# Pairing the 64-row low-weight passes of two column groups on the two row halves of TensorE

## The chip, the cores and the metric

The kernel runs on one core of a Trainium2 chip. The metric is the device time in microseconds of one execution. Engines: PE (TensorE, matmul), PEld (its weight loads, which overlap PE), DVE (VectorE), ACT (ScalarE), POOL (GpSimd) and SP (the queue that issues most transfers).

## The reference

An adaptive layer norm block over 2048 tokens of 576 channels: a long convolution (S4D), then a feed-forward network with a hidden width of 4608. Cut to what matters:

```python
def _B_ref(x, w1, w2):
    h = jnp.einsum("bsd,df->bsf", x, w1)
    zero = jnp.zeros_like(h)
    h = jnp.maximum(h, zero)
    return jnp.einsum("bsf,fd->bsd", h, w2)

x = A_u
mod = (_silu(c) @ w_mod).reshape(c.shape[0], 6, 1, -1)
sa, ca, ga, sb, cb, gb = (mod[:, 0], mod[:, 1], mod[:, 2], mod[:, 3], mod[:, 4], mod[:, 5])
h = _layernorm(x, axis=-1) * (1 + ca) + sa
x = x + ga * _A_ref(h, A_log_A_real, A_A_imag, A_C_real, A_C_imag, A_log_dt, A_D_skip)
h = _layernorm(x, axis=-1) * (1 + cb) + sb
x = x + gb * _B_ref(h, B_w1, B_w2)
return x
```

`_A_ref` is the convolution with a kernel of 2048 taps for each channel, done with FFTs. Everything is float32.

## The kernel before

**Stages.** The kernel first makes the convolution's taps and the first block's convolution (`conv0`). From about 209 us on it works on four blocks of 512 tokens: the feed-forward network of block b runs on PE, and between its passes stand, in portions, the convolution and norm of block b+1 (generators that `step`, L1405, advances four times per column group: once inside `first`, once after it, once inside `second`, once at the end of the iteration). A portion holds up to some 2.7 us of DVE work by the kernel's own figures. DVE, ACT and PE each run their instructions in the order in which they were issued; a scheduler orders them by program order and by when they become ready in its own model.

**Feed-forward.** The hidden width is cut into 36 column groups of 128, so there are 4 × 36 = 144 groups g. For each, `first(g)` (L1362) makes the 128 × 512 sum `hps` (hidden columns × tokens) and `second(g)` (L1379), two iterations later, multiplies it by w2 into five accumulators. To keep float32 accuracy, both operands are split into a high and a low part in fp32r, and three products are made: high × high, high weight × low activation, low weight × high activation.

**The tail of 64 channels.** 576 is 4 × 128 + 64. For the four full chunks `first` runs three passes each. The host stores the last 64 rows of w1 twice, in partitions 0 to 63 and 64 to 127 of the fifth chunk; `norm2` (L1074) makes the activations of those channels in both halves too. The tile `xs` holds the high part in partitions 0 to 63 and the low part in 64 to 127 (L1128 to L1132). So one pass with the high weights, over all 128 rows, makes high × high and high × low at once. The second pass, with the low weights, is over 128 rows as well. That is 14 passes per group: 2 with `xs`, 12 with `xh` and `xl`.

**After the sum.** ACT makes `hh = relu(hps)` (L1375), DVE makes `hl = max(hps, 0) − hh` (L1376). `hps` has two buffers, so `first(g + 2)` can't start before `hl(g)` has read its own. `hh` and `hl` have three buffers each.

**Weights.** `load_r1` and `load_r2` (L1319 and on) bring the raw weights; ACT makes the high parts (`split1`, L1337; `split2`, L1350), DVE the low parts in block 0, which are saved to DRAM; later blocks load them back (`low1`, L1327, for w1; in `split2` for w2). The buffers of `w1` are three; that of group g was free after `first(g)`, and `low1(g + 3)` was issued there. The transfers go through SP's queue in program order.

Of the kernel before, what the change touches and what calls it, by code (L numbers as in the profile page):

```python
# [10 lines left out]
F32 = mybir.dt.float32  # L11
F32R = mybir.dt.float32r
I32 = mybir.dt.int32
AF = mybir.ActivationFunctionType
ALU = mybir.AluOpType
# [3 lines left out]
P = 128  # L19
# [5 lines left out]
NF = F // P  # L25
# [503 lines left out]
class Body:  # L529
# [20 lines left out]
    def v(self, *args, **kw):  # L550
        return self.kept(self.nc.vector.tensor_tensor(*args, **kw))  # L551
# [522 lines left out]
    def norm2(self, s, x2, xp, st=None):  # L1074

        nc, v = self.nc, self.nc.vector.tensor_tensor
        xh = xp.tile([P, 4, 512], F32R, tag="xh", bufs=1, name=f"xh_{s}")
        xl = xp.tile([P, 4, 512], F32R, tag="xl", bufs=1, name=f"xl_{s}")
        xs = xp.tile([P, 512], F32R, tag="xs", bufs=1, name=f"xs_{s}")
        self.xT[s] = (xh, xl, xs)  # L1080
        if st is None:
            st = self.sums("st2")
            for p in range(2):
                yield from self.stats(
                    lambda i: x2[:, i, p * PC : (p + 1) * PC], [t[:, p] for t in st]
                )
        rs = self.norms(st, False)
        yield 2.0
        if s == 0:
            h2 = [self.cv.tile([P, D + 64], F32, tag="h2", bufs=4, name="h2") for _ in range(4)]  # L1090
        else:
            h2 = [
                t[:, i * (D + 64) : (i + 1) * (D + 64)]
                for t in (self.spec(f"h2_{i}").rearrange("p a b c -> p (a b c)") for i in range(2))
                for i in range(2)
            ]
        for n2 in range(4):
            if s == 0 and n2 % 2 == 0:
                self.kept(nc.vector.tensor_scalar(
                    h2[n2][:, :D], x2[:, n2], rs[n2][:, 0:1], rs[n2][:, 3:4],  # L1100
                    op0=ALU.subtract, op1=ALU.mult,
                ))
                self.kept(nc.scalar.activation(h2[n2][:, D:], h2[n2][:, 512:D], AF.Copy))
                continue
            for a, b, c in ((0, D, 0), (512, D, D)):
                self.kept(nc.scalar.activation(
                    h2[n2][:, c : c + b - a], x2[:, n2, a:b], AF.Identity,
                    scale=rs[n2][:, 3:4], bias=rs[n2][:, 4:5],
                ))
        yield -1  # L1110
        if s:
            xfs = self.spec("xf").rearrange("p a b c -> p (a b c)")[:, :2048]
            xfs = xfs.rearrange("p (i t) -> p i t", i=4)
        for kk in (4, 0, 1, 2, 3):
            ps = self.cps.tile([P, 4, P], F32, tag="cps", bufs=self.nps, name="ps_t")
            for n2 in range(4):
                nc.tensor.transpose(ps[:, n2], h2[n2][:, kk * P : (kk + 1) * P], self.ident)
            if s == 0:
                xf = self.cv.tile([P, 512], F32, tag="xf", bufs=2, name="xf")
            else:  # L1120
                xf = xfs[:, kk % 4]
            ps = ps.rearrange("p a b -> p (a b)")
            cb, sb = (self.m[n][:, kk : kk + 1] for n in ("cb", "sb"))
            if s == 0 and kk in (0, 2):
                nc.vector.tensor_scalar(xf, ps, cb, sb, op0=ALU.mult, op1=ALU.add)
            else:
                nc.scalar.activation(xf, ps, AF.Identity, scale=cb, bias=sb)
            hi = xs if kk == 4 else xh[:, kk]  # L1128
            a = nc.scalar.activation(hi, xf, AF.Copy)  # L1129
            yield None  # L1130
            if kk == 4:
                d = v(xs[64:P], xf[64:P], xs[64:P], op=ALU.subtract)  # L1132
            else:
                d = v(xl[:, kk], xf, hi, op=ALU.subtract)  # L1134
            yield 0.7
        self.ends = a.ins, d.ins

    def conv0(self, ctx, c, kg, first, late):

        nc, tc, I = self.nc, self.tc, self.I  # L1140
# [23 lines left out]
        def load(t, a):  # L1164
            return self.kept(nc.sync.dma_start(out=t, in_=a))
# [15 lines left out]
        for t, a in ((fcKn, I["neg"][0]), (self.gc, I["gc"]), (gcn, I["neg"][1])):  # L1181
            d = load(t, a)
# [35 lines left out]
        g = lambda n2, c: self.gc[:, n2, c, :]  # L1218
# [16 lines left out]
        def back(p, ops, order=(0, 2, 1, 3)):  # L1235
            for i in order:
                for w in self.inverse(x2, p, ops, (i,)):
                    if w is None:
                        yield
                self.kept(nc.vector.bn_stats(out=st[i][:, p], in_=xv[:, i, :, p]))  # L1240
# [12 lines left out]
        odd = [back(0, ops(V), (i,)) for i in (1, 3)]  # L1253
# [18 lines left out]
        self.ff = self.pool(ctx, "ff", side="right")  # L1272
        next(self.start)
        self.xp = [self.pool(ctx, "xa", side="right")]
        with tc.issue_after(self.mact.ins):
            next(self.start)
        W = S(0, "W")
# [10 lines left out]
        n = 0  # L1288
# [22 lines left out]
    def ffn(self, gens):  # L1311

        nc, I, ff = self.nc, self.I, self.ff
        v = self.v
        n = NB * NF
        r1, r2, w1, w2 = {}, {}, {}, {}
        late = []

        def load_r1(g):  # L1319
            r1[g] = ff.tile([P, 5, P], F32, tag="r1", bufs=3, name="r1")  # L1320
            self.kept(nc.sync.dma_start(out=r1[g], in_=I["w1"][g % NF]))
# [5 lines left out]
        def low1(g):  # L1327
            w = w1[g] = ff.tile([P, 2, 5, P], F32R, tag="w1", bufs=3, name="w1")
            if g >= NF:
                nc.sync.dma_start(  # L1330
                    out=w[:, 1].rearrange("p k c -> p (k c)").bitcast(F32), in_=self.L1d[g % NF]
                )
# [27 lines left out]
                nc.sync.dma_start(out=w[:, D:].bitcast(F32), in_=self.L2d[g % NF])  # L1360

        def first(g):  # L1362
            xh, xl, xs = self.xT[g // NF]
            w = w1.pop(g)
            ps = self.fps.tile([P, 512], F32, tag="hps", bufs=2, name="hps")
            ops = [(w[:, 0, 4], xs), (w[:, 1, 4], xs)]
            for k in range(4):
                ops += [(w[:, 0, k], xh[:, k]), (w[:, 0, k], xl[:, k]), (w[:, 1, k], xh[:, k])]
            for i, (a, x) in enumerate(ops):
                nc.tensor.matmul(ps, a, x, start=(i == 0), stop=(i == 13))  # L1370
                if i == 6:
                    step(g)
            hh = ff.tile([P, 512], F32R, tag="hh", bufs=3, name="hh")
            hl = ff.tile([P, 512], F32R, tag="hl", bufs=3, name="hl")
            nc.scalar.activation(hh, ps, AF.Relu)  # L1375
            nc.vector.scalar_tensor_tensor(hl, ps, 0.0, hh, op0=ALU.max, op1=ALU.subtract)  # L1376
            return hh, hl

        def second(g, hh, hl):  # L1379
            f = g % NF  # L1380
# [24 lines left out]
        def step(g):  # L1405

            at[0] += 1
            at[1] = g
            target = self.rate(g // NF) * (at[0] % 144 or 144)
            gen = gens[g // NF]  # L1410
            v = pe = 0.0
            room = (9.0, 7.0, 7.0, 7.0)[g // NF] - sum(recent[-3:])
            recent.append(0.0)
            while done[0] < target and v < min(room, 2.7) and pe < 2:
                w = next(gen, 0)
                if gen.gi_frame is None or w == -1:
                    return
                if w is None:
                    pe += 1
                    done[0] += 0.7  # L1420
                else:
                    v += w
                    recent[-1] = v
                    done[0] += w
# [14 lines left out]
        split2(0)  # L1439
        split1(1)  # L1440
        yield
        waiting = []
        for g in range(n + 2):
            if g < n:
                if g + 3 < n:
                    load_r1(g + 3)
                if g + 2 < n:
                    load_r2(g + 2)
                for dst, src in late:
                    nc.sync.dma_start(out=dst, in_=src.bitcast(F32))  # L1450
                late.clear()
                if g:
                    split2(g)
                if g and g + 2 < n:
                    split1(g + 2)
                waiting.append((g, *first(g)))
                if g == 0:
                    split1(2)
                if g + 3 < n:
                    low1(g + 3)  # L1460
                step(g)
            if g > 1:
                e = waiting[0][0]
                second(*waiting.pop(0))
                if e % NF == NF - 1 and e < n - 1:
                    self.evacuate(e // NF)
            if g == 2:
                yield
            if g < n:
                step(g)  # L1470
                if g % NF == NF - 1:
                    for _ in gens[g // NF]:
                        pass
                    done[0] = 0.0
# [151 lines left out]
```

## Time and profile before

| | us |
|---|---|
| median of 3 runs | 1341.48 (1340.31 to 1343.99) |
| profiled execution | 1337.9 |
| its span, first to last instruction | 1336.1 |
| PE busy | 1216.4 |
| DVE busy | 869.5 |
| ACT busy | 503.7 |
| start of the feed-forward stage | about 209 |

A row of instructions in the profile reads: line, engine, operation, output and inputs, shape, count; then the busy time in us and the mean of one in ns; then the idle time of the engine just before them and what ended it. A timeline row has the start and the length of a run of instructions ahead of that, and in brackets the idle time before it. "Issue" as a releaser means that the engine waited for nothing that the profile shows. `128*64` and the like after a matmul's tiles are the active rows and columns of the array. A matmul's recorded end is modelled, and passes overlap in the records.

### The profile page before, as it was taken

To read this page: it belongs to the slowest core of one execution; us is meant where nothing else is said; L and a number is where in the kernel's file an instruction comes from. 1 tells how busy PE (TensorE), PEld (TensorE's weight loads), DVE (VectorE), ACT (ScalarE), POOL (GpSimd) and SP (SyncE) were. 2 spreads that over 40 slices of the span, in tenths; PEclk is the share of its full clock that TensorE was granted. 3 is DMA by queue.
4 is the path that set the end of the run, shared out by engine and by line. 5 is a ranking of instruction groups with operands and counts; after the bars stand their busy time and mean duration, and the time that the engine had idled before them with its cause. 6 is when DMAs were issued, how large, how long until landed. Compare 5 with 4: busy or idle time off the path is not lost.

```text
span 1336.1 us, 26046 instructions
## 1 busy us (share of the span) xinstructions
PE 1216.4 (91%) x10608; PEld 970.6 (73%) x10608; DVE 869.5 (65%) x1351; ACT 503.7 (38%) x1014; POOL 194.5 (15%) x273
## 2 busy tenths in 40 slices
PE   5035788999999998999999998999999999999998
PEld 3024666788787786778777786777888888888886
DVE  5999978999887898389457885367998222111111
ACT  7987225222224322522243235433323353223331
POOL 1788231111120000111111100100010000000000
PEclk9557899999999998999999999999999999999999
DMA  6668499888898876698779893868897556666651
GB/s 199 238 241 283 163 347 404 290 294 308 284 357 279 291 254 208 227 391 319 250 251 338 288 362 111 277 180 281 310 358 226 172 181 213 199 197 197 197 167 62
DMA packets 132456, 340.47 MB, mean 255 GB/s; under 512 B 22384, under 2 KB 22704, under 8 KB 132336
## 3 DMA queue, kind: packets, MB, share of 16 engines
q1 hardware_dynamic: 105200, 215.21, 48.8%
q0 software_dynamic: 26848, 123.01, 25.1%
q8 instruction: 83, 1.36, 0.4%
q10 hardware_dynamic: 288, 0.59, 0.1%
q14 instruction: 37, 0.30, 0.1%
HBM read 258.55 MB, written 80.22 MB: 254 GB/s over the span
## 4 chain that ended last, share of the span: by engine, by line
PE 73%; DVE 15%; DMA 4%; issue 3%; ACT 3%; POOL 2%; ACTq 0%; DVEq 0%; POOLq 0%
PE hps L1370 30%; PE acc L1395 30%; PE kps L481 5%; PE ps_f L803 4%; DVE T L551 3%; DVE Y L551 2%; DVE W L551 2%; POOL W L59 2%; PE ps_i L1064 2%; PE kps L648 1%; DMA Ka<-Rd 1%; DMA Ua<-Ud 1%; DVE k L139 1%; DVE T L254 1%; DVE V L551 1%
## 5 line engine op out<-in xcount | busy, mean ns | idle before, releaser
L1395 PE MATMUL acc<-hh,w 128*128 128x512 f32 x1296 | 421.6, 399 | 2.1 <-DVE w L551 2.0
L1370 PE MATMUL hps<-xh,w 128*128 128x512 f32 x1152 | 393.9, 402 | 0.8 <-ACT xh L1129 0.4
L1395 PEld LDWEIGHTS acc<-hh,w 128*128 128x128 f32 x1296 | 243.1, 189 | 55.1 <-DVE w L551 2.8
L1376 DVE SCALAR_TENSOR_TENSOR hl<-hps,hh 128x512 fp32r<-128x512 f32 x144 | 98.8, 686 | 279.3 <-ACT hh L1375 279.1
L1395 PE MATMUL acc<-hl,w 128*128 128x512 f32 x720 | 280.5, 399 | 0.0
L1370 PEld LDWEIGHTS hps<-xh,w 128*128 128x128 f32 x1152 | 217.1, 189 | 48.6 <-ACT xh L1129 1.8
L1370 PE MATMUL hps<-xl,w 128*128 128x512 f32 x576 | 230.2, 400 | 0.2 <-DVE xl L1134 0.2
L1375 ACT ACTIVATE hh<-hps 128x512 fp32r<-128x512 f32 x144 | 86.1, 598 | 336.3 <-PE hps L1370 331.7
L1348 ACT ACTIVATE w<-r 128x576 fp32r<-128x576 f32 x144 | 98.7, 686 | 235.5 <-issue 179.8
L1395 PEld LDWEIGHTS acc<-hl,w 128*128 128x128 f32 x720 | 135.7, 189 | 28.1
L1370 PEld LDWEIGHTS hps<-xl,w 128*128 128x128 f32 x576 | 109.2, 190 | 25.0 <-DVE xl L1134 1.7
L269 PE MATMUL kps<-W,W 128*32 128x16 f32 x2304 | 40.3, 215 | 73.9 <-POOL W L59 49.5
L1341 ACT ACTIVATE w<-r 128x640 fp32r<-128x640 f32 x142 | 104.0, 732 | 6.8 <-DVE hl L1376 4.0
L1370 PE MATMUL hps<-xs,w 128*128 128x512 f32 x288 | 97.6, 419 | 3.1 <-DVE hl L1376 2.9
L269 PEld LDWEIGHTS kps<-W,W 128*32 128x32 f32 x2304 | 37.8, 150 | 79.4 <-POOL W L59 50.8
L551 DVE TENSOR_TENSOR Y<-Y,T 128x1152 f32<-128x1152 f32 x64 | 84.9, 1350 | 0.1
L481 PEld LDWEIGHTS kps<-W1r,W2r 128*32 128x32 f32 x3456 | 63.8, 146 | 24.5 <-issue 19.3
L481 PE MATMUL kps<-W1r,W2r 128*32 128x48 f32 (+2 forms) x3456 | 71.0, 237 | 5.9 <-issue 5.8
L804 ACT ACTIVATE Z<-ps_f 128x288 f32<-128x288 f32 x104 | 42.4, 407 | 66.3 <-PE ps_f L803 64.1
L1370 PEld LDWEIGHTS hps<-xs,w 128*128 128x128 f32 x288 | 53.7, 192 | 16.2 <-DVE hl L1376 4.3
L551 DVE TENSOR_TENSOR W<-Z 128x576 f32<-128x576 f32 x52 | 37.0, 752 | 41.2 <-ACT Z L804 41.2
L551 DVE TENSOR_TENSOR w<-r,w 128x512 fp32r<-128x512 f32 (+2 forms) x108 | 57.9, 571 | 2.9 <-ACT w L1348 2.9
(216 smaller groups left out, 1360.6 us busy)
## 6 DMA issues: line engine op xcount, KB each, us to landing
r<-in_w_dram SPq DMA_DIRECT2D x144, 320.0 KB, 4.2
r<-in_w_dram SPq DMA_DIRECT2D x144, 288.0 KB, 3.7
w<-L1d SPq DMA_DIRECT2D x108, 320.0 KB, 3.0
w<-L2d SPq DMA_DIRECT2D x108, 288.0 KB, 3.1
W2r<-W2d POOLq DMA_DIRECT2D x18, 1536.0 KB, 9.0
W2d<-W SPq DMA_DIRECT2D x10, 1536.0 KB, 7.4
W<-W1d POOLq DMA_DIRECT2D x18, 768.0 KB, 9.0
Ua<-Ud POOLq DMA_DIRECT2D x12, 1152.0 KB, 10.5
```

Of the source, the lines that this page charges most:

```text
L59: self.tc.keep_in_program_order(self.nc.gpsimd.tensor_tensor(out, a, b, op=op))
L269: self.nc.tensor.matmul(ps[32 * dd : 32 * dd + 32, 12 * u + q, :], W2[:, r, :, ch], W1[:, u, :, r, ch], start=(r == 0), stop=(r == 1),)
L481: nc.tensor.matmul(ps[32 * dd : 32 * dd + 32, q, :], W2[:, r, :, ch], W1[:, :na, r, ch], start=(r == 1), stop=(r == 0),)
L551: return self.kept(self.nc.vector.tensor_tensor(*args, **kw))
L803: kept(nc.tensor.matmul(o, fc[:, n2, c, :], src(n2), start=True, stop=True))
L804: nc.scalar.activation(Z[:, n2, c], ps[:, :PC], AF.Copy)
L1341: nc.scalar.activation(w[:, 0], r, AF.Copy)
L1348: nc.scalar.activation(w[:, 0:D], r2[g], AF.Copy)
L1370: nc.tensor.matmul(ps, a, x, start=(i == 0), stop=(i == 13))
L1375: nc.scalar.activation(hh, ps, AF.Relu)
L1376: nc.vector.scalar_tensor_tensor(hl, ps, 0.0, hh, op0=ALU.max, op1=ALU.subtract)
L1395: nc.tensor.matmul(acc[i], a, x, start=(f == 0 and j in (0, 3, 6, 9, 12)), stop=(f == NF - 1 and j in (2, 5, 8, 11, 13)),)
```

## The change

The low-weight pass of the tail now covers 64 rows only (low weight × high activation). Those of two neighbouring groups are put side by side: that of the even group on array rows 0 to 63, that of the odd group on rows 64 to 127, each into its own `hps`. For that, the high part of the activations must also lie in partitions 64 to 127: a new tile `xd` holds it. `first` keeps 13 passes. The even group's sum is closed, and evicted (`hh`, `hl`), by the pair that stands at the head of the odd group's iteration (`halves`); the odd group's sum is opened there. The weight buffer of an even group is held until then, and the `low1` calls move accordingly.

```diff
@@ norm2
-        self.xT[s] = (xh, xl, xs)
+        xd = self.xd.tile([P, 512], F32R, tag=f"xd{s % 2}", bufs=1, name=f"xd_{s}")
+        self.xT[s] = (xh, xl, xs, xd)
...
-            hi = xs if kk == 4 else xh[:, kk]
-            a = nc.scalar.activation(hi, xf, AF.Copy)
+            if kk == 4:
+                nc.scalar.activation(xd[64:P], xf[64:P], AF.Copy)
+                a = nc.scalar.activation(xs[0:64], xf[0:64], AF.Copy)
+            else:
+                hi = xh[:, kk]
+                a = nc.scalar.activation(hi, xf, AF.Copy)
             yield None
             if kk == 4:
-                d = v(xs[64:P], xf[64:P], xs[64:P], op=ALU.subtract)
+                d = v(xs[64:P], xf[64:P], xd[64:P], op=ALU.subtract)
...
@@ conv0
+        self.xd = self.pool(ctx, "xd", side="right")
...
@@ ffn
         def first(g):
-            xh, xl, xs = self.xT[g // NF]
-            w = w1.pop(g)
-            ps = self.fps.tile([P, 512], F32, tag="hps", bufs=2, name="hps")
-            ops = [(w[:, 0, 4], xs), (w[:, 1, 4], xs)]
+            xh, xl, xs, _ = self.xT[g // NF]
+            w = w1[g]
+            odd = g % 2
+            ps = hps[g] if odd else self.fps.tile([P, 512], F32, tag="hps", bufs=2, name="hps")
+            hps[g] = ps
+            ops = [(w[:, 0, 4], xs)]
             for k in range(4):
                 ops += [(w[:, 0, k], xh[:, k]), (w[:, 0, k], xl[:, k]), (w[:, 1, k], xh[:, k])]
             for i, (a, x) in enumerate(ops):
-                nc.tensor.matmul(ps, a, x, start=(i == 0), stop=(i == 13))
+                nc.tensor.matmul(
+                    ps, a, x, start=(i == 0 and not odd), stop=(i == 12 and bool(odd))
+                )
                 if i == 6:
                     step(g)
+            if odd:
+                evict(g)
+
+        def evict(g):
+            del w1[g]
+            ps = hps.pop(g)
             hh = ff.tile([P, 512], F32R, tag="hh", bufs=3, name="hh")
             hl = ff.tile([P, 512], F32R, tag="hl", bufs=3, name="hl")
             nc.scalar.activation(hh, ps, AF.Relu)
             nc.vector.scalar_tensor_tensor(hl, ps, 0.0, hh, op0=ALU.max, op1=ALU.subtract)
-            return hh, hl
+            waiting.append((g, hh, hl))
+
+        def halves(g):
+            _, _, xs, xd = self.xT[g // NF]
+            ps = hps[g] = self.fps.tile([P, 512], F32, tag="hps", bufs=2, name="hps")
+            nc.tensor.matmul(hps[g - 1], w1[g - 1][0:64, 1, 4], xs[0:64], start=False, stop=True)
+            nc.tensor.matmul(ps, w1[g][64:P, 1, 4], xd[64:P], start=True, stop=False)
+            evict(g - 1)
...
         for g in range(n + 2):
+            if g % 2 and g < n:
+                halves(g)
+                if 1 < g + 2 < n:
+                    low1(g + 2)
             if g < n:
...
-                waiting.append((g, *first(g)))
+                first(g)
                 if g == 0:
                     split1(2)
-                if g + 3 < n:
+                if g % 2 and g + 3 < n:
                     low1(g + 3)
                 step(g)
```

More of the change, by code (lines that the diff above doesn't have):

```diff
@@ L1441, in ffn @@
         yield
-        waiting = []
+        waiting, hps = [], {}
         for g in range(n + 2):
+            if g % 2 and g < n:
+                halves(g)
+                if 1 < g + 2 < n:
+                    low1(g + 2)
             if g < n:
```

## The prediction

> **What bounds the kernel now.** I read the shares of busy time first, then the same by block of 512 tokens, then the chain of work that ended last in the last block.
>
> ```profile
> PE 1216.4 (91%) x10608; PEld 970.6 (73%) x10608; DVE 869.5 (65%) x1351; ACT 503.7 (38%) x1014; POOL 194.5 (15%) x273
> ...
> PE 73%; DVE 15%; DMA 4%; issue 3%; ACT 3%; POOL 2%; ACTq 0%; DVEq 0%; POOLq 0%
> ...
> L1370 PE MATMUL hps<-xs,w 128*128 128x512 f32 x288 | 97.6, 419 | 3.1 <-DVE hl L1376 2.9
> ```
> ```profile
> 209.00:545.00 336.00, 324.21 (x3444) 255.99 (x3444) 291.90 (x392) 106.63 (x201) 40.32 (x59) 0.98 0.82 289
> 545.00:827.00 282.00, 277.37 (x2250) 219.71 (x2249) 202.15 (x259) 91.58 (x170) 32.83 (x46) 0.99 0.84 293
> 827.00:1089.00 262.00, 261.91 (x1158) 210.17 (x1158) 165.98 (x233) 100.67 (x179) 14.62 (x20) 1.00 0.74 245
> 1089.00:1328.00 239.00, 239.00 (x1070) 197.57 (x1069) 30.07 (x46) 71.80 (x113) 2.20 (x4) 1.00 0.59 178
> ```
> ```profile
> by line: PE acc L1395 49.4%; PE hps L1370 49.4%; PE ps_o L1533 0.9%; PE ps_o L1539 0.4%
> ...
> 1130.57 3.17 PE hps L1370 x14
> ```
>
> The second fence has the four blocks of the feed-forward stage, columns: window, length, then busy time of PE, PEld, DVE, ACT, POOL, granted clock, DMA share, GB/s. PE is busy for all but 0.1 us of the last two blocks, but idle for 11.8 us of block 0 (336.00 − 324.21) and 4.6 us of block 1, where DVE is busiest (291.90 of 336). The third fence is the chain between 1100 and 1300 us: nothing but PE. So a change in PE's work counts in full, and in block 0 something else sometimes ends last. Fourteen passes follow one another in 3.17 us: **one pass slot is 3.17 / 14 = 0.226 us** (a single pass lasts longer in the records, 419 ns on average in the L1370 row, but the next starts before it ends).
>
> **The change on PE.** Each column group issues one low-weight tail pass, over 128 rows. There are 144 (L1370 counts two passes with xs a group, x288). They go: 144 × 0.226 = −32.6 us. In their place stand 72 pairs of 64-row passes. A pair that truly runs side by side takes one slot: 72 × 0.226 = +16.3. Alone that makes −16.3 us, the whole prize.
>
> Against it stands the change of array shape, 128 rows to 64 and back. The trace has this, at the start of the kernel, where the modulation product (L648) closes each sum over 128-row passes with a 64-row pass. The weight loads (PEld) show it:
>
> ```profile
> 22.11 0.92 PEld L648 LDWEIGHTS kps<-wm_ca,cb 128*128 128x128 f32 x4
> ...
> 23.41 0.29 PEld L648 LDWEIGHTS kps<-wm_ca,cb 64*128 64x128 f32 x2 [0.39 <-issue]
> 24.09 1.75 PEld L648 LDWEIGHTS kps<-wm_ca,cb 128*128 128x128 f32 x8 [0.39 <-issue]
> 26.23 0.29 PEld L648 LDWEIGHTS kps<-wm_ca,cb 64*128 64x128 f32 x2 [0.39 <-issue]
> ...
> L1395 PEld LDWEIGHTS acc<-hh,w 128*128 128x128 f32 x1296 | 243.1, 189 | 55.1 <-DVE w L551 2.8
> ```
>
> A load takes 0.19 us (last row). In an undisturbed run four loads take 0.92 us, so they start (0.92 − 0.19) / 3 = 0.243 us apart, each under the pass before it. Before the first 64-row load and before the first 128-row load after it, the loader stands idle for 0.39 us and waits for nothing recorded: the load isn't pulled ahead, it starts when the passes of the other shape are through, and the next pass then waits for it. From 23.41 to 26.23 lie ten loads in 2.82 us; ten in a row would take 2.43. **In and out of the 64-row shape costs 0.39 us.** The Trainium skill's page "TensorEngine Tiling (Array Packing)", Key Properties, says that "Changing tiling mode (not just tile) drains the TensorE", without a figure; by that rule too the change is charged twice a pair, and the trace agrees (0.39 us a round trip).
>
> Those passes are fp32, the feed-forward ones fp32r. The column-split passes of the convolution (L481, 32 columns) come in between fp32r passes:
>
> ```profile
> 330.49 0.19 PEld L1370 LDWEIGHTS hps<-xl,w 128*128 128x128 f32 x1
> 331.03 0.21 PEld L481 LDWEIGHTS kps<-W1r,W2r 128*32 128x32 f32 x8 [0.35 <-issue]
> ...
> 237.74 2.31 PE L481 MATMUL kps<-W1r,W2r 128*32 128x48 f32 x96
> ...
> L481 PE MATMUL kps<-W1r,W2r 128*32 128x48 f32 x1152 | 27.8, 266 | 0.1
> ```
>
> The load after an fp32r pass is late in the same way (0.35 us idle; 0.54 after the load before it instead of 0.226). So I charge 72 × 0.39 = +27.9 us (unrounded 0.387). The price is bounded by zero (the load pulled ahead after all) and by this.
>
> How far two 64-row halves overlap has no row. The nearest are the last two: 96 passes of the four column strips in 2.31 us, 0.024 us each, though one lasts 0.266: tiles of one shape do run at once, and eight of their loads take 0.21 us together. So I take full overlap. Between: the second load starts 0.10 us after the first as in the 64-row rows (0.29 − 0.19), +7.4 us. Upper end: none, a second slot, +16.3 us. **PE's own sum: −32.6 + 16.3 + 27.9 = +11.6 us**, between −16.3 (free switch) and +27.9 (no overlap).
>
> **The change on DVE: a later release.** hps has two buffers; the group two further on may start when DVE's hl (L1376) has read the sum. Before, hl(g) is issued right after group g's passes. After, an even group's sum is closed by the pair at the head of the next iteration, so its hl stands on DVE behind three more portions of convolution work (the steps after first, inside second and at the end). Where DVE runs level with PE that costs nothing:
>
> ```profile
> 1280.39 0.69 DVE L1376 SCALAR_TENSOR_TENSOR hl<-hps,hh 128x512 fp32r<-128x512 f32 x1 [5.65 <-ACT hh L1375]
> 1286.73 0.69 DVE L1376 SCALAR_TENSOR_TENSOR hl<-hps,hh 128x512 fp32r<-128x512 f32 x1 [5.66 <-ACT hh L1375]
> ```
>
> There DVE waits 5.65 of 6.34 us per group. It costs where PE already waits for hl, and PE does so at two places:
>
> ```profile
> 231.00 0.73 PE L1370 MATMUL hps<-xs,w 128*128 128x512 f32 x2 [1.46 <-DVE hl L1376]
> ...
> 510.63 1.80 PE L1395 MATMUL acc<-hh,w 128*128 128x512 f32 x5 [1.96 <-DVE w L551]
> 513.83 1.23 PE L1370 MATMUL hps<-xs,w 128*128 128x512 f32 x2 [1.41 <-DVE hl L1376]
> ```
> ```profile
> 230.27 0.68 DVE L1376 SCALAR_TENSOR_TENSOR hl<-hps,hh 128x512 fp32r<-128x512 f32 x1
> 230.87 1.75 DVE L449 TENSOR_TENSOR T<-W1r,Zr 128x1536 f32<-128x1536 f32 x1
> ...
> 237.61 0.21 DVE L551 TENSOR_TENSOR w<-r,w 128x64 fp32r<-128x64 f32 x1
> ```
> ```profile
> 513.10 0.68 DVE L1376 SCALAR_TENSOR_TENSOR hl<-hps,hh 128x512 fp32r<-128x512 f32 x1
> 513.70 2.75 DVE L551 TENSOR_TENSOR W<-Y 128x576 f32<-128x576 f32 x4
> 516.37 2.89 DVE L551 TENSOR_TENSOR V<-W 128x576 f32<-128x576 f32 x6
> 519.18 1.55 DVE L551 TENSOR_TENSOR w<-r,w 128x64 fp32r<-128x64 f32 x3
> ```
>
> Counted from the start, the hl at 230.27 is that of group 2 and the one at 513.10 that of group 32, both even. Up to the next weight split (w<-r), which opens the next iteration, lie 230.87 to 237.61 = 6.7 us of DVE work, and 513.70 to 519.18 = 5.5 us. With hl behind it, group 4 starts 6.7 us later and group 34 5.5 us later. PE runs in order, so what stands behind the waiting pass (second(2) and the L481 passes at 237.74) waits as well. I take both in full: **+12.2 us**. Lower end 0 (DVE's order comes out otherwise, or PE catches up in waits that lie behind). Upper end 15.3: a long idle spell also slows the clock:
>
> ```profile
> 513.83 6.23 PE hps L1370 x14
> ...
> 513.80:520.00 6.20, 6.17 (x15) 4.92 (x16) 6.20 (x13) 0.00 (x0) 0.00 (x0) 0.52 0.36 138
> ```
>
> After the idle spells around 510 the granted clock is 0.52 and fourteen passes take 6.23 us instead of 3.17; the same once more behind group 4 would be 3.1 us.
>
> **The rest.** norm2's kk = 4 copy on ACT becomes two, of 64 partitions each:
>
> ```profile
> 206.69 0.63 ACT L1129 ACTIVATE xs<-xf 128x512 fp32r<-128x512 f32 x1
> ...
> 208.13 0.78 ACT L1127 ACTIVATE xf<-ps_t,m_sb,m_cb 128x512 f32<-128x512 f32 x1 [0.30 <-DVE xs L1132]
> ...
> 212.62 0.50 PE L1370 MATMUL hps<-xl,w 128*128 128x512 f32 x1 [0.23 <-DVE xl L1134]
> ```
>
> At the start PE waits for the last xl, so the extra copy (0.63 us, the row's price for the same length) shows once: +0.6, between 0 and 2.5 (four blocks). ACT's hh of an even group moves one second() later; its splits for the next groups stand behind it and have a group's time. On SP, the low-weight load of an odd group now waits for the pair, and the r loads queue behind it:
>
> ```profile
> r<-in_w_dram SPq DMA_DIRECT2D x144, 320.0 KB, 4.2
> ...
> w<-L1d SPq DMA_DIRECT2D x108, 320.0 KB, 3.0
> ```
>
> The r load, 4.2 us, is read one group (6.34 us) later, the L1d load, 3.0 us, two groups later: nothing, while PE's group hides them. Without that cover an r load 4.2 us late would delay ACT's copy alone, needed two groups on.
>
> **Sum:** 11.6 + 12.2 + 0.6 = +24.4 us. The profiled execution took 1337.9 us (span 1336.1), 3.6 below the median of the runs, 1341.5; the forecast is 1362.3 for such an execution and **1365.9 for the median**.
>
> **Rivals.**
> 1. The late hl does no harm: DVE's order places it earlier, or PE makes up for it. For: PE waits for hl only 1.46 and 1.41 us there. Against: those waits end last. 1341.5 + 11.6 + 0.6 = 1353.7.
> 2. The halves don't run side by side, so the change doesn't do what it says: 27.9 + 12.2 + 0.6, 1382.2. For: no row shows two row halves at once.
> 3. Faster: with half the rows free, the second half's load, and the load back to 128 rows, go under a running pass, so the switch is free: −16.3 + 0.6 makes 1325.8, with the late hl 1338.0. It decides from a round trip below 0.226 us a pair. Against: the idle 0.39 and 0.35 us above. The Trainium skill's page "TensorE: Matmul & The Clock Gate", Part 3, The mechanism, names a span of one pass and about 4 ns more per tile, and no switch; by it alone this rival would hold. No run here shows row halves.
>
> **Chances.** Forecast 0.50; rival 1 0.22; rival 2 0.16; rival 3 0.12, half of it faster than 1337.5 and half, with the late hl, within 0.3% (about what a measurement can tell from no change). Faster 0.06, same 0.06, slower 0.88. The range goes from rival 1 less 3.7 us (pairs that fall into PE's waits, no norm2 cost), 1350, to rival 2 with the slow clock, 1385; rival 3 is left out.
>
> **What would show it.** In the changed profile: PEld idle some 0.35 us before the pair's first load and before the load behind it, in all four blocks; the two halves' starts under 0.02 us apart (0.10 or 0.23 means rival 2's side); a pair of groups in the last block 0.16 us longer than 2 × 6.34; PE waits of 5 to 9 us for hl near 231 and 513. It would be wrong if the loads were pulled ahead, or if hl of groups 2 and 32 kept its place.

## The result and the profile after

| us | before | after |
|---|---|---|
| median | 1340.26 (6 runs, 1338.38 to 1343.99) | 1363.47 (6 runs, 1358.78 to 1368.89) |
| profiled execution (its span) | 1337.9 (1336.1) | 1359.43 (1357.7) |

The ratio is 1.0164 [1.0139, 1.0188]: the change makes the kernel slower by 1.6%, some 22 us, beside the 24.4 us forecast. The two profiled spans differ by 21.6 us. All times and ratios here are of fast executions; one slow execution each of the switch kernel (2423.86 us) and of before with the fix (3655.75 us) is left out.

The page of the kernel after, busy time and the one full-height tail pass that is left:

```profile
PE 1235.3 (91%) x10608; PEld 954.2 (70%) x10608; DVE 870.2 (64%) x1351; ACT 500.2 (37%) x1018; POOL 194.6 (14%) x273
...
L1379 PE MATMUL hps<-xs,w 128*128 128x512 f32 x144 | 68.0, 472 | 3.5 <-DVE hl L1394 2.9
```

PE has exactly as many passes as before (10608: two 64-row passes stand where two 128-row passes stood), but is busy for 18.9 us longer. So most of the loss lies in PE's own stream (where a slow clock counts, too), not in waits. The passes with `xs` (x144 instead of x288) last 472 ns on average instead of 419.

The four blocks of the kernel after, in the view of busy time by window (columns as in the prediction):

```profile
209.00:549.00 340.00, 329.39 (x3451) 252.14 (x3450) 293.37 (x394) 107.15 (x204) 40.39 (x59) 0.98 0.81 285
549.00:837.00 288.00, 281.98 (x2246) 215.43 (x2245) 201.81 (x259) 91.15 (x172) 32.87 (x46) 0.99 0.81 286
837.00:1110.00 273.00, 269.56 (x1167) 208.52 (x1166) 165.85 (x232) 99.20 (x178) 14.63 (x20) 0.99 0.70 239
1110.00:1349.00 239.00, 239.00 (x1051) 190.02 (x1051) 29.87 (x46) 68.61 (x112) 2.20 (x4) 1.00 0.54 175
```

Block 2, in which PE was idle for 0.1 us before, is 11 us longer and idle for 3.4 us (273.00 − 269.56). Nothing in the prediction speaks of that. The windows are set by eye; the exact lengths below run from the first pass with `xh` of a block to that of the next (in the last block to the last pass with `acc`).

| block length, us | 0 | 1 | 2 | 3 |
|---|---|---|---|---|
| before | 331.9 | 287.1 | 261.1 | 237.4 |
| after | 334.4 | 293.1 | 270.8 | 241.1 |
| after less before | +2.5 | +6.0 | +9.7 | +3.7 |

The pairs alone should give the same in each block. Block 3, where nothing waits, shows what they give: +3.7. Block 2 holds 6 us more than that; block 0, where the whole +12.2 us for the late hl had been placed, holds less (though block 0 varies by 5 us from profile to profile, as the repeats below show).

Where the pair stands, the timeline of PE and that of its weight loads (start, length, instruction, idle before), kernel after, last block:

```profile
1193.48 0.39 PE L1421 MATMUL acc<-hl,w 128*128 128x512 f32 x1
1193.80 0.50 PE L1401 MATMUL hps<-xs,w 64*128 64x512 f32 x1
1193.81 0.50 PE L1402 MATMUL hps<-xd,w 64*128 64x512 f32 x1
1194.23 0.50 PE L1379 MATMUL hps<-xs,w 128*128 128x512 f32 x1
1194.57 0.40 PE L1379 MATMUL hps<-xh,w 128*128 128x512 f32 x1
```
```profile
1193.26 0.19 PEld L1421 LDWEIGHTS acc<-hl,w 128*128 128x128 f32 x1
1193.80 0.18 PEld L1401 LDWEIGHTS hps<-xs,w 64*128 64x128 f32 x1 [0.35 <-issue]
1193.80 0.18 PEld L1402 LDWEIGHTS hps<-xd,w 64*128 64x128 f32 x1
1194.23 0.19 PEld L1379 LDWEIGHTS hps<-xs,w 128*128 128x128 f32 x1 [0.24 <-issue]
1194.34 0.19 PEld L1379 LDWEIGHTS hps<-xh,w 128*128 128x128 f32 x1
```

Both mechanisms that the prediction named are there. The halves start together, and so do their loads (both at 1193.80). And the loader stands idle for 0.35 us before the pair and 0.24 us behind it. From 1193.48 to 1194.57 lie 1.09 us for what would be three slots, 0.68 us: in and out of the 64-row shape costs 0.41 us here. Over the whole kernel, the page of waits of the weight loads sums it:

```profile
PEld hps L1401 <- issue: 24.0, 68, 0.4
...
PEld hps L1379 <- issue: 17.5, 71, 0.4
```

24.0 us over 68 of the 72 pairs, 0.35 each, and 17.5 us over 71, 0.25 each.

Not every pair looks like this one. In 65 of the 72 the halves start 0.01 us apart or less. In six, all in blocks 0 and 1, the scheduler put 1 to 99 other passes between the halves, and in a seventh, in block 0, the second half waits 1.82 us for hl. A split pair pays two ways in and out and has no overlap. The loads of that of groups 34 and 35, with nine full-height passes between:

```profile
522.82 0.18 PEld L1401 LDWEIGHTS hps<-xs,w 64*128 64x128 f32 x1 [0.37 <-issue]
523.24 1.92 PEld L1421 LDWEIGHTS acc<-hh,w 128*128 128x128 f32 x9 [0.24 <-issue]
525.53 0.18 PEld L1402 LDWEIGHTS hps<-xd,w 64*128 64x128 f32 x1 [0.36 <-DVE x L551]
525.95 0.19 PEld L1379 LDWEIGHTS hps<-xs,w 128*128 128x128 f32 x1 [0.24 <-issue]
```

The prediction counted on 72 pairs side by side.

### The profile page after: what moved, and what is told of

The parts are those of the page before. It is cut to its first block, busy times and chain, and to the rows that moved or that the text cites. A ratio compares the mean times of both kernels' runs of the same rounds, so it can differ in the third digit from the quotient of the medians.

```text
span 1357.7 us, 26017 instructions
## 1 busy us (share of the span) xinstructions
PE 1235.3 (91%) x10608; PEld 954.2 (70%) x10608; DVE 870.2 (64%) x1351; ACT 500.2 (37%) x1018; POOL 194.6 (14%) x273
## 5 line engine op out<-in xcount | busy, mean ns | idle before, releaser
L1379 PE MATMUL hps<-xh,w 128*128 128x512 f32 x1152 | 406.4, 406 | 0.4 <-ACT xh L1134 0.4
L1379 PE MATMUL hps<-xs,w 128*128 128x512 f32 x144 | 68.0, 472 | 3.5 <-DVE hl L1394 2.9
L804 ACT ACTIVATE Z<-ps_f 128x288 f32<-128x288 f32 x104 | 42.5, 409 | 73.7 <-PE ps_f L803 73.4
L59 POOL TENSOR_TENSOR W<-c,E 128x384 f32<-128x384 f32 (+1 forms) x48 | 45.9, 995 | 27.4 <-ACT c L56 27.4
```

The source lines that it names most:

```text
L59: self.tc.keep_in_program_order(self.nc.gpsimd.tensor_tensor(out, a, b, op=op))
L804: nc.scalar.activation(Z[:, n2, c], ps[:, :PC], AF.Copy)
L1379: nc.tensor.matmul(ps, a, x, start=(i == 0 and not odd), stop=(i == 12 and bool(odd)))
```

## The experiments

**One part alone: the order, the switch, the overlap.** Three kernels, measured on one chip. The first keeps everything of the change but the 64-row shape: both low-weight passes of the pair go over all 128 rows, back to back, at the pair's place.

```diff
-            nc.tensor.matmul(hps[g - 1], w1[g - 1][0:64, 1, 4], xs[0:64], start=False, stop=True)
-            nc.tensor.matmul(ps, w1[g][64:P, 1, 4], xd[64:P], start=True, stop=False)
+            nc.tensor.matmul(hps[g - 1], w1[g - 1][:, 1, 4], xs, start=False, stop=True)
+            nc.tensor.matmul(ps, w1[g][:, 1, 4], xs, start=True, stop=False)
```

> The order of the change without the change of shape: the two low-weight passes of the pair run over all 128 rows again, one after the other, at the place of the pair, so the eviction of the even group stays late. Theory A (as predicted: the late hl costs PE 12.2 us at two places): 12 to 13 us over before, ratio about 1.009. Theory B (the late hl is filled with other passes; what the change costs beyond the pairs' 13 us is one wait of PE for ACT in block 2 of about 5 us, and that comes from where the scheduler puts the norm): 0 to 6 us over before, and no net idle time of PE gained in block 0.

Measured: 1354.03 us, 1.008 [1.0053, 1.0108] of before. So the order and the norm cost about 0.8%, 10.7 us, beside 12.8 forecast for them (12.2 + 0.6); the rest of the change's 1.64%, 0.84% or 11.3 us, belongs to the pairs, beside 11.6 forecast. By size both terms hold, give or take some 5 us when both intervals are taken together; the 0 to 6 us of theory B were missed. The place doesn't hold; that comes below.

The second is the kernel before with a switch and nothing to gain: the low-weight pass of each even group covers 64 rows. It leaves out the product of low weight and low activation in the tail of the even groups.

```diff
-            ops = [(w[:, 0, 4], xs), (w[:, 1, 4], xs)]
+            low = (w[:, 1, 4], xs) if g % 2 else (w[0:64, 1, 4], xs[0:64])
+            ops = [(w[:, 0, 4], xs), low]
```

> Before, with the low-weight tail pass of the even groups over 64 rows in place of 128, alone and in its old place: 72 changes of shape in and out, the same number of passes, the same order. (It leaves out the low x low product of the even groups' tail.) If the switch costs 0.39 us a round trip, as read from the modulation product: 27.9 us over before, ratio 1.021, spread evenly over the four blocks. If the switch were free for fp32r passes: no change.

Measured: 1365.05 us, 1.0171 [1.0131, 1.021]: 23.0 us over before (17.6 to 28.2), or 0.32 us a round trip. The profiled span grew from 1336.1 to 1363.2, 27.1 us, or 27.1 / 72 = 0.376 us; 0.387 had been charged. It isn't spread evenly, as had been expected: the blocks grew by 9.8, 3.9, 6.2 and 6.7 us. The cleanest reading is the last block, where nothing else waits. The 36 hl of that block, count with first and last start, before and then in this kernel:

```profile
L1376 DVE SCALAR_TENSOR_TENSOR hl<-hps,hh x36: 691/692/693, 1093.1 to 1318.5; 128x512 fp32r<-128x512 f32 x36
```
```profile
L1377 DVE SCALAR_TENSOR_TENSOR hl<-hps,hh x36: 690/692/693, 1113.6 to 1345.6; 128x512 fp32r<-128x512 f32 x36
```

225.4 us became 232.0: 6.6 us for 17 switches (the one of the block's first group lies ahead of its hl), 0.39 us each. The switch is real, and fp32r passes pay what the fp32 passes at the kernel's start do. Rival 3 (free) is out.

The third puts both halves on the same 64 rows: the switch stays, the overlap goes.

```diff
-            nc.tensor.matmul(ps, w1[g][64:P, 1, 4], xd[64:P], start=True, stop=False)
+            nc.tensor.matmul(ps, w1[g][0:64, 1, 4], xs[0:64], start=True, stop=False)
```

> The change with both halves on array rows 0 to 63: same switches, same order, but the two 64-row passes can't run at once. If the halves overlap fully in the change: one slot more a pair, 72 x 0.226 = 16.3 us over the change, some 38 us over before. If they did not overlap there: no difference from the change.

Measured: 1369.69 us, 1.0204 [1.0168, 1.0239]. That is only some 6 us above the kernel after, where a slot a pair, 16.3 us, was to be lost. Again the last block tells it. The first half of each pair in the last block, count with first and last start, in the order-only kernel, the kernel after and this one:

```profile
L1401 PE MATMUL hps<-xs,w x18: 389/389/477, 1106.6 to 1325.6; 128*128 128x512 f32 x18
```
```profile
L1401 PE MATMUL hps<-xs,w x18: 498/498/498, 1113.3 to 1335.7; 64*128 64x512 f32 x18
```
```profile
L1401 PE MATMUL hps<-xs,w x18: 493/493/494, 1115.2 to 1341.3; 64*128 64x512 f32 x18
```

Seventeen pairs of groups take 219.0, 222.4 and 226.1 us. So a pair side by side costs 3.4 / 17 = **0.20 us more than two plain passes**, and a pair on the same rows another 3.7 / 17 = 0.22 us, one slot. The halves do run side by side, and rival 2 is out. Over the whole kernel the lost slot doesn't show in full: this kernel's blocks 0 and 1 are 333.6 and 294.1 us long, −0.8 and +1.0 beside after. Whether these blocks take it up in their waits or block 0's variation hides it was not settled.

**Where the order's cost lies.** The order-only kernel's blocks are 330.3, 291.9, 267.8 and 237.6 us: beside before that is 6.7 us more in block 2, 4.8 in block 1, less in block 0 and nothing to speak of in block 3. What ends PE's idle time there, in the view of waits between 837 us and the end of the block, is one line, first in the kernel after, then in the order-only kernel; before has no such line.

```profile
PE ps_f L803 <- ACT Z L804: 3.4, 1, 3.4
```
```profile
PE ps_f L803 <- ACT Z L804: 3.8, 1, 3.8
```

Z (L804) is a convolution product that ACT copies out of PSUM, eight times in this stretch; PE makes the next one when the copy is through. ACT's timeline around it, before:

```profile
861.56 0.41 ACT L804 ACTIVATE Z<-ps_f 128x288 f32<-128x288 f32 x1 [0.84 <-PE ps_f L803]
862.97 0.41 ACT L804 ACTIVATE Z<-ps_f 128x288 f32<-128x288 f32 x1 [1.00 <-PE ps_f L803]
865.83 0.85 ACT L865 ACTIVATE mv<-mv,eps 128x1 f32<-128x1 f32 x4 [2.44 <-DVE mv L864]
866.58 0.39 ACT L804 ACTIVATE Z<-ps_f 128x288 f32<-128x288 f32 x1
```

and after, with DVE's row that the roots (L865) wait for, and what PE does:

```profile
871.16 0.41 ACT L804 ACTIVATE Z<-ps_f 128x288 f32<-128x288 f32 x1 [0.84 <-PE ps_f L803]
875.42 0.85 ACT L865 ACTIVATE mv<-mv,eps 128x1 f32<-128x1 f32 x4 [3.84 <-DVE mv L864]
876.18 0.38 ACT L804 ACTIVATE Z<-ps_f 128x288 f32<-128x288 f32 x1
877.41 0.41 ACT L804 ACTIVATE Z<-ps_f 128x288 f32<-128x288 f32 x1 [0.84 <-PE ps_f L803]
```
```profile
872.30 2.98 DVE L849 BATCH_NORM_STATS2 st<-x 128x6 f32<-128x288 f32 x8 [7.21 <-DMA x<-in_x_dram]
```
```profile
872.85 0.39 PE L1379 MATMUL hps<-xh,w 128*128 128x512 f32 x1
876.62 0.75 PE L803 MATMUL ps_f<-kt,fcK 128*128 128x288 f32 x2 [3.38 <-ACT Z L804]
...
878.11 1.05 PE L1421 MATMUL acc<-hh,w 128*128 128x512 f32 x2
```

Before, the four roots of the norm stand behind the seventh Z, and only the eighth waits for them; PE has no product left that needs it. After, they stand behind the sixth. They wait for DVE's sums, DVE for a load of x, and the seventh Z stands in the queue behind them. The next product (876.62) needs its buffer, and the passes behind it in PE's queue wait as well: 3.38 us. It doesn't end there. The granted clock behind the idle spell, windows of the kernel after:

```profile
873.30:876.60 3.30, 0.00 (x0) 0.00 (x0) 3.30 (x16) 1.14 (x5) 0.00 (x0) 1.00 0.63 234
```
```profile
877.50:880.60 3.10, 3.10 (x9) 2.43 (x8) 3.10 (x7) 0.32 (x1) 1.16 (x1) 0.52 0.26 67
```

Nine passes in 3.10 us, at 0.52 of the clock; at full clock they would take 2.0 (9 × 0.226). So the slow spell costs at least another 1 us.

I tried two ways to take that wait away. The first starts the norm two portions later:

```diff
-            yield from both(self.norm1(x2, h), mm_K(0, ZK))
+            yield from both(after(2, self.norm1(x2, h)), mm_K(0, ZK))
```

> The change with the norm of blocks 2 and 3 begun two turns later beside the transform of the taps, so that ACT reaches the roots, which wait for DVE's statistics, behind the last copies of the transform. Theory B: the PE wait of 3.4 us for ACT's Z in block 2 and the slow clock after it go, about 5 us less than the change, some 17 us over before. Theory A, in which that wait plays no part: within 1 us of the change.

A miss: 1368.41 us, 1.0188 [1.0157, 1.0218], and the wait in block 2 grew to 5.2 us in one piece. A shift of the program order didn't move the roots behind the seventh Z; the scheduler still placed them ahead of it.

The second says what is meant: an order of ACT's instructions (no semaphore) puts each of these roots behind the last Z issued. It was added to the kernel after, to the order-only kernel and to the kernel before.

```diff
-                nc.scalar.activation(Z[:, n2, c], ps[:, :PC], AF.Copy)
+                self.z = nc.scalar.activation(Z[:, n2, c], ps[:, :PC], AF.Copy)
...
                 self.kept(sq)
+                if not self.pinned:
+                    self.tc.add_manual_dep(
+                        sq.ins, self.z.ins.name,
+                        mybir.DependencyInfo(
+                            mybir.DependencyClass.NoSync, mybir.DependencyReason.DATA
+                        ),
+                        reason="behind",
+                    )
```

> The change with ACT's order fixed at one place: the roots of a norm stand behind the last copy of the transform that was issued before them. Theory B2 (PE's wait of 3.4 us for ACT's Z in block 2, and the slow clock behind it, are part of what the change costs): that wait goes, about 5 us less than the change, some 18 us over before. Theory A (the cost beyond the pairs is the late hl alone): within 1 us of the change.

> The same fix in the kernel that has the order of the change with full-row passes, which took 11 us over before. Theory B2: half of it goes, 5 to 6 us over before stay, as PE waits in block 1. Theory A: 11 us stay.

> Control: the same fix in the kernel before, where PE doesn't wait for ACT's Z in block 2. Both theories: within 2 us of before.

Measured: after with the fix 1358.49 us, 1.0151 [1.0122, 1.018]; order-only with the fix 1342.56, 1.0036 [1.0014, 1.0059]; before with the fix 1340.95, 1.0006 [0.9985, 1.0027]. The wait is gone. The same stretch of block 2, kernel after and kernel after with the fix:

```profile
868.00:883.00 15.00, 11.62 (x43) 8.39 (x42) 10.50 (x29) 3.42 (x11) 1.16 (x1) 0.89 0.64 231
```
```profile
868.00:883.00 15.00, 15.00 (x64) 11.38 (x64) 9.73 (x28) 6.50 (x15) 1.16 (x1) 1.00 0.95 323
```

In the same 15 us PE makes 64 passes instead of 43, and the clock stays at 1.00. Block 2 shrinks from 270.8 to 266.0 us; in the order-only kernel from 267.8 to 262.7, 1.6 above before. Before has nothing to gain from the fix, since its roots stood right. So the fix takes back only what the new order had lost.

By the median, after with the fix was no clear gain over after's own (1.0151 against 1.0164, on different chips). So three kernels went to one chip again: after, after with the fix, order only.

> The change itself once more, beside its fixed and its full-row variants on one chip. Theory B2: 20 to 24 us over before; of these 15 from the pairs, 5 from ACT's order in block 2, the rest from the order in blocks 0 and 1.

> The change with the roots behind the transform's last copy, again, since the interval of the first time overlapped that of the change. Theory B2: 4 to 6 us less than the change beside it. If the wait in block 2 were made up for later: within 1.5 us of it.

> The order of the change with full-row passes, again, on the same chip as the change. Pairs at 0.205 us each: 15 us less than the change, 6 to 10 us over before.

| same chip, before 1341.08 | us | ratio | blocks 0 to 3 |
|---|---|---|---|
| after | 1365.87 | 1.0163 [1.0141, 1.0185] | 339.6, 294.1, 272.8, 241.1 |
| after with the fix | 1358.36 | 1.0115 [1.0083, 1.0147] | 336.1, 291.7, 266.3, 241.1 |
| order only | 1353.98 | 1.0079 [1.0051, 1.0106] | 336.2, 289.7, 268.0, 237.6 |

The fix is worth 0.48%, 6.4 us, by the ratios; the order-only kernel's two ratios (with the fix 1.0036 on another chip) give 0.44%. The 64-row shape costs 0.84% once more, 11.3 us. The Z wait comes back in block 2 of both kernels without the fix (4.1 and 4.2 us in one piece) and not in the one with it (0.3 us for another reason). Blocks 2 and 3 repeat to within 2 us; block 0 of one kernel differs by 5 to 6 us from profile to profile (334.4 and 339.6; 331.0 and 336.1; 330.3 and 336.2), so a term of a few microseconds can't be read from one block 0.

**The pair earlier.** The last one lets the pair follow right behind the even group's passes, so that its hl goes back to its old place; for that, the odd group's buffer must be free one iteration earlier.

```diff
-            if g % 2 and g < n:
-                halves(g)
-                if 1 < g + 2 < n:
-                    low1(g + 2)
             if g < n:
...
                 first(g)
+                if g % 2 == 0:
+                    halves(g + 1)
                 if g == 0:
                     split1(2)
-                if g % 2 and g + 3 < n:
+                if g + 3 < n:
                     low1(g + 3)
```

> The change with the pair right behind the even group's own passes, so that the even group's hl keeps its old place on DVE; the odd group's buffer is needed one second() earlier instead. If the place of hl behind DVE's convolution work makes the order cost: the pairs' price alone remains, 0.205 x 72 = 15 us over before, about 8 less than the change. If the shorter time between hl and the next use of its buffer makes it: no better than the change, with PE waiting for hl of the odd groups in blocks 0 and 1.

Measured: 1356.83 us, 1.0152 [1.012, 1.0185], the same as after with the fix; by the ratio 20.4 us over before, where 15 had been expected. Its block 2 is 264.7 us long without any Z wait: another order, and the roots happen to fall right. Block 0 of its profile, 345.4 us, is the longest of all. That execution was its slowest (1366.39), but its rows show something else as well: in 12 of the 18 pairs of block 0 the scheduler put other passes, 7 to 206 of them, between the two halves, and PE waits 3.0 us for hl at one of the second halves. So this run can't tell what moving hl back is worth: what it gained may have gone into the split pairs. No kernel beat the kernel before.

## Why the prediction was right, and where it wasn't

The forecast, 1365.9 us, stands 2.4 us above the measured 1363.47. Step by step:

- **The prize and the switch: right in kind, a little off in size.** A pair was to cost 0.387 − 0.226 = 0.16 us; it costs 0.20 by the last block (219.0 to 222.4 us for 17; the repeats give 219.0 and 222.4 again), or 14.4 us for 72 instead of 11.6. By the timed runs it is 11.3 us twice and 15.4 between the two kernels with the fix (1.0151 − 1.0036), each give or take some 5 us. The loader's idle time is 0.35 us before the pair, as forecast, and 0.24 behind it instead of 0.35. The difference in the price is in the way in and out: 0.41 us a pair by the rows above instead of 0.387, with another 0.01 before the pass after it. Why a pair pays some 0.04 us more than the single 64-row pass of the switch experiment (0.39) was not followed up. The six split pairs had no place in the sum: at 0.226 + 0.39 us for each lone half against 2 × 0.226 before, one would cost 0.78 us instead of 0.20, so up to 3.5 us together. That is an estimate from these rows; no run isolates it, and where PE doesn't set the pace it costs less.
- **Full overlap: right, though its row didn't show it.** In 65 pairs the halves start 0.01 us apart or less, under the 0.02 set as the mark, and the same-rows kernel pays one slot more a pair. The Trainium skill's page "TensorE: Matmul & The Clock Gate", Part 3, The mechanism, has about 4 ns more per tile; the trace agrees (0.003 us in the median pair). The prediction took full overlap from 96 passes of 48 columns, 0.024 us each. That row says little: at 0.226 us for 512 columns, 48 columns take 0.021 us (an estimate), so passes that merely follow one another would look the same. Full overlap was a guess that came true. What told the sign was the switch, read from the idle 0.39 us of before's own trace.
- **The late hl: the step that failed.** The prediction took "both in full: **+12.2 us**", at groups 4 and 34. The order did cost 10.7 us, but elsewhere and for another reason, so the close sum owes something to luck. What it said of hl came true. The kernel after, PE's rows around the first wait for hl, and DVE's rows from hl of group 2 on:

```profile
225.82 0.79 PE L1402 MATMUL hps<-xd,w 64*128 64x512 f32 x1 [1.82 <-DVE hl L1394]
...
235.60 2.20 PE L1421 MATMUL acc<-hh,w 128*128 128x512 f32 x9
...
240.62 0.50 PE L1379 MATMUL hps<-xs,w 128*128 128x512 f32 x1
...
260.32 0.39 PE L1379 MATMUL hps<-xs,w 128*128 128x512 f32 x1
```
```profile
238.24 0.68 DVE L1394 SCALAR_TENSOR_TENSOR hl<-hps,hh 128x512 fp32r<-128x512 f32 x1
...
244.32 1.75 DVE L451 TENSOR_TENSOR W1r<-W,Zr 128x1536 f32<-128x1536 f32 x1
...
527.94 0.64 DVE L1394 SCALAR_TENSOR_TENSOR hl<-hps,hh 128x512 fp32r<-128x512 f32 x1
```

hl(2) moved from 230.27 to 238.24, behind the portions listed in the prediction, and group 4 began at 240.62 instead of 231.00, 9.6 us late. But DVE's stream was hardly late: these are DVE's rows of the kernel before, then PE's, then the windows:

```profile
230.27 0.68 DVE L1376 SCALAR_TENSOR_TENSOR hl<-hps,hh 128x512 fp32r<-128x512 f32 x1
...
243.25 1.76 DVE L451 TENSOR_TENSOR W1r<-W,Zr 128x1536 f32<-128x1536 f32 x1
...
526.20 0.64 DVE L1376 SCALAR_TENSOR_TENSOR hl<-hps,hh 128x512 fp32r<-128x512 f32 x1
```
```profile
251.98 0.67 PE L481 MATMUL kps<-W1r,W2r 128*32 128x16 f32 x30 [2.69 <-issue]
...
260.20 0.61 PE L1370 MATMUL hps<-xs,w 128*128 128x512 f32 x2
```
```profile
226.00:258.00 32.00, 27.23 (x456) 21.63 (x455) 31.92 (x32) 6.43 (x12) 4.73 (x7) 0.95 0.86 314
498.00:523.00 25.00, 21.53 (x81) 16.67 (x80) 25.00 (x37) 5.69 (x9) 0.00 (x0) 0.86 0.44 141
```

DVE is busy for 31.92 of the 32 us from 226 to 258 in the kernel before (third number behind the length), PE for 27.23. DVE is what sets the pace there; this is read from the rows, no run isolates it. A move of hl among DVE's work adds nothing to that work: the same product starts at 243.25 before and at 244.32 after, 1.07 us later (1.6 counted from the block's first pass), not 9.6. PE used the time for other passes (the nine at 235.60 among them), and before's idle 2.69 us at 249.3 doesn't come after. Two groups on the delay is gone: group 6 begins at 260.20 before and at 260.32 after. At the second place it is much the same: DVE is busy for all of the 25 us around it (last row), group 34 begins 3.7 us late (517.52 instead of 513.83) after a wait of 1.10 us, before's fourteen passes at half clock (6.23 us, quoted in the prediction) run at full clock after, and a little later hl is 1.7 us late (526.20 and 527.94). The error was to add a wait of PE in full in a stretch that PE doesn't set. The window row that shows this is quoted in the prediction for the whole block (291.90 of 336); read for the stretch itself, it would have put this term far below 12 us. The waits of "5 to 9 us for hl" that were to be seen aren't there: the longest of PE's is 1.8 us.
- **What took its place, not predicted:** the roots ahead of the seventh Z on ACT in block 2. Shown, by the fix: the wait goes, and block 2 is 4.8 to 6.5 us shorter in each of the three comparisons of profiles. In the timed runs the fix is worth 0.48% on one chip, and across chips 0.44% and 0.13%, so its size is less sure: some 5 us of the order's 10.7. That the scheduler's own model makes this order because the work around it was issued in another sequence is argued; why it falls so wasn't settled. What is left, 0.36% or 4.8 us [1.9 to 7.9] in the order-only kernel with the fix, is not isolated: its blocks 1 and 2 are 1.2 and 1.6 us longer than before's (0.0 and 1.0 us longer than those of before with the fix). In the order-only kernel without the fix PE does wait for hl in block 1 (2.4 us in three pieces), which speaks for the late hl there, but no run takes that alone away.
- **norm2's extra copy: +0.6,** too small to be told apart; it is in the order-only kernels.
- **Rivals.** 1 (the late hl harmless, 1353.7) had the mechanism right at the two places named, and the sum wrong, because the new order hurt in block 2. After with the fix, 1358.4, is the nearest to it that was run. 2 and 3 fell by the same-rows and the switch kernel.

## What to carry to other kernels

One 64-row pass beside another saves one pass slot, 0.226 us here, and the way into and out of the 64-row shape costs 0.4 us. By these numbers at least two such pairs of 512 columns would have to share one switch to gain anything; no run here tried it. Look in the trace whether the two halves still stand together: the scheduler split six of 72 pairs here. A later release adds its wait only where the waiting engine sets the pace of that stretch; read the busy time of all engines in the very stretch, not in the block. After any change of issue order compare the order of each engine's instructions, since an unrelated copy behind a waiting one (here ACT's seventh Z) can cost several us, some 5 here beside the pairs' 11 to 15.

## What the runs showed of the hardware that was not expected

- A 64-row pass costs the same to enter and leave among fp32r passes (0.39 us in the last block) as among fp32 ones (0.39).
- The weight loads of two row halves run side by side, too: both at 1193.80, 0.18 us each, where 0.10 us between them had been allowed for.
- An idle spell of 3.38 us was followed by 0.52 of the clock for some 3 us, so a wait on PE costs more than its length. The Trainium skill's page "TensorE: Matmul & The Clock Gate", Part 1, puts the clock at half rate after an idle window of about 3.4 us. The trace agrees for this spell, but shorter ones were followed by 0.52 as well: 1.96 and 1.41 us, with five passes between, in the rows at 510.63 and 513.83 that the prediction quotes.
